# First gate weights on two hardware queues, with one x chunk on GpSimd's queue

## The chip, the cores and the metric

The kernel runs on one core of a Trainium2 chip. The metric is the device time of one execution in microseconds (us), lower is better. The kernel before takes 204.66 us (median of 5 runs, 204.03 to 205.20).

## The reference

The input x is 2048 rows of 512 (bf16). It is layer-normalized, and then two layers work on the same normalized rows; their outputs are added to x.

```python
def _B_ref(x, w1, w3, w2):              # gated layer, F = 1792
    gate = jnp.einsum("bsd,df->bsf", x, w1)
    up = jnp.einsum("bsd,df->bsf", x, w3)
    return jnp.einsum("bsf,fd->bsd", _silu(gate) * up, w2)

x = A_x
xn = _layernorm(x, axis=-1)
# _A_ref: complex state-space layer: Bu = x @ B_bar, scan h = Lam_bar * h + Bu, y = 2 Re(h @ C) + x * Dskip
return x + _A_ref(xn, ...) + _B_ref(xn, B_w1, B_w3, B_w2)
```

## The kernel before, in words

The 2048 rows are worked on in 4 blocks of 512 rows; a block is 4 chunks of 128 rows. F = 1792 is cut into 14 gate tiles of 128 columns. For a block the gated layer (`glu`) runs, for each gate tile f, four matmuls with w1 (the 512 inputs are 4 tiles of 128) and four with w3 into two PSUM tiles; ScalarE copies them out (`evac`: SiLU for the gate, a plain copy for the other), VectorE multiplies. The state-space layer (`bu`, `ssm_tasks`) and the output products (`y_fast`) follow between and behind.

Each engine runs its instructions in the order in which the program writes them. VectorE's work between the matmuls is placed by a small planner (`Filler`), whose costs and due times the change doesn't touch.

Block 0 has a start of its own, since nothing is loaded yet. Its rows come chunk by chunk, and its first three gate tiles (`FIRST` = 3) are computed chunk by chunk too, by `quarter`, line 557: `quarter(0, (0, 1), 2)` is chunk 0 with gate tiles 0 and 1, first all of w1, then all of w3, 16 matmuls of 128 columns. For each chunk, VectorE makes mean and variance (`ln_stats`, lines 214 and 215), ScalarE the inverse deviation (`ln_first_rstd`, 228 and 229), VectorE normalizes (`ln_apply`, 219), TensorE transposes (`ln_first_transpose`, 238) and ScalarE copies the transposed tile out (239). TensorE warms up before that with matmuls on constants (`keep_busy`, 191).

The order of TensorE's work in the start is written out by hand:

```python
quarter(0, (0, 1), 2)
quarter(1, (0, 1))
pps = params_transpose()
...
ln_first_transpose(2)
quarter(0, (2,))
ln_first_transpose(3)
quarter(1, (2,))
```

`params_transpose` (line 310) transposes the state-space layer's parameter rows, which GpSimd loads in three small DMAs (line 200); ScalarE and GpSimd derive small tables from them, and VectorE the angle tables (369 to 372). From gate tile 3 on, whole blocks are multiplied (line 525).

Loads: SyncE and ScalarE each issue half of x chunks 0 and 1 (line 161). Then ScalarE issues chunk 3 (162) and SyncE chunk 2 (163). `load_w(f0, f1)` loads columns f0 to f1 of w1 (line 151) and of w3 (152): first 0 to 256, gate tiles 0 and 1, then 256 to 512, gate tiles 2 and 3; all on SyncE. A load of 256 columns is 256 KB, a chunk of x 128 KB. GpSimd has a queue of its own, of the software kind, on which it also runs its accumulating DMAs. `bulk_loads` (the rest of w1 and w3, block 1 of x, the transposed loads of B and C) starts on SyncE once the first chunk's deviation is there, and `late_loads` (w2, Dskip, blocks 2 and 3 of x) come at about 33 us.

Of the kernel before, what the change touches and what calls it, by code (L numbers as in the profile page):

```python
# [17 lines left out]
P = 128  # L18
# [45 lines left out]
def kernel(  # L64
# [17 lines left out]
    nc = tc.nc  # L82
# [23 lines left out]
    xv = A_x[0].rearrange("(c p) d -> p c d", p=P)  # L106
# [39 lines left out]
    x_blk = [xpool.tile([P, CPB, D], BF16, name="x_blk") for _ in range(NBLK)]  # L146
# [3 lines left out]
    def load_w(f0, f1, eng1=nc.sync, eng3=nc.sync):  # L150
        eng1.dma_start(out=w1_sb[:, :, f0:f1], in_=w1v[:, :, f0:f1])  # L151
        eng3.dma_start(out=w3_sb[:, :, f0:f1], in_=w3v[:, :, f0:f1])

    def load_x(b, parts=1):
        n = CPB // parts
        for i in range(0, CPB, n):
            nc.sync.dma_start(out=x_blk[b][:, i:i + n, :], in_=xv[:, b * CPB + i:b * CPB + i + n, :])

    for c in range(2):
        for eng, dsl in ((nc.sync, slice(0, D // 2)), (nc.scalar, slice(D // 2, D))):  # L160
            eng.dma_start(out=x_blk[0][:, c, dsl], in_=xv[:, c, dsl])  # L161
    nc.scalar.dma_start(out=x_blk[0][:, 3, :], in_=xv[:, 3, :])
    nc.sync.dma_start(out=x_blk[0][:, 2, :], in_=xv[:, 2, :])  # L163
    load_w(0, 2 * P)
    load_w(2 * P, 4 * P)

    def bulk_loads():
# [9 lines left out]
    def late_loads():  # L177
        nc.sync.dma_start(out=w2_sb, in_=B_w2.rearrange("(t p) d -> p t d", p=P))
        nc.sync.dma_start(out=dskip_row, in_=A_Dskip.partition_broadcast(P))
        load_x(2, 4)  # L180
        load_x(3)


    ones = nc.const_aps.tensor(1.0, (P, TBLK), BF16)
# [615 lines left out]
    for t in ln1b:  # L800
        bg.add(*t, ("ln", 1))
    bg.add(0.0, late_loads, ("ln", 1))
    bg.add(0.2, params_w)
    gate = glu(0)
# [94 lines left out]
```

## Time and profile before

| | before |
|---|---|
| median of 5 runs | 204.66 us (204.03 to 205.20) |
| profiled execution, its own time | 204.66 us |
| profiled execution, span of its instructions | 202.8 us |
| TensorE (PE) busy | 198.1 us, 98% of the span |
| VectorE (DVE) busy | 172.5 us, 85% |
| ScalarE (ACT) busy | 125.4 us, 62% |
| GpSimd (POOL) busy | 41.5 us, 20% |
| granted TensorE clock | full speed in every slice |
| first w1 load: issued, landed | 2.11, 5.79 us |
| first w3 load: issued, landed | 2.58, 7.60 us |
| second w1 load and w3 load: issued | 3.13 and 3.69 us |

All times in the profile count from the start of the span. A DMA's time to landing runs from its issue to the completion that its reader waits for. `PEld` is the loading of weights into TensorE, which overlaps the matmuls; `SPq` and `ACTq` are DMA issues by SyncE and ScalarE. The DMA engines are 16, shared by all queues. Matmuls are pipelined, so a matmul's start tells more than its duration: consecutive starts of the 128-column matmuls lie about 0.056 us apart.

### The profile page before, as it was taken

How to read it: one execution, taken by the hardware profiler on the slowest of the kernel's cores; microseconds unless marked ns; L12 is line 12 of the kernel's file. 1: busy time of each engine (PE TensorE's matmuls, PEld its weight loads, DVE VectorE, ACT ScalarE, POOL GpSimd, SP SyncE). 2: the span in 40 equal slices, each digit the busy share in tenths (PEclk: the TensorE clock that was granted, in tenths of full speed). 3: DMA queues.
4: the chain of work that ended last, by engine and by line, in shares of the span. 5: the costliest groups of instructions: out<-in, count | busy, mean ns of one | idle time of the engine just before them, and what ended most of it. 6: DMA issues, size and time to landing. Idle time of an engine off the chain costs nothing.

```text
span 202.8 us, 3451 instructions
## 1 busy us (share of the span) xinstructions
PE 198.1 (98%) x1317; PEld 122.8 (61%) x1317; DVE 172.5 (85%) x242; ACT 125.4 (62%) x251; POOL 41.5 (20%) x68
## 2 busy tenths in 40 slices
PE   8899999999999999999999999999999999999994
PEld 2774444444444588854444445888444458888993
DVE  4589699999999999989949999999999935584832
ACT  4699897699999976969766676110576662101010
POOL 7070269700310043041111010310101110000000
PEclk9999999999999999999999999999999999999999
DMA  5999986992483043936796004466330780101011
GB/s 157 327 249 209 298 166 116 324 266 46 91 156 66 0 83 68 169 99 118 75 187 128 13 13 94 93 141 133 90 65 0 150 162 1 52 3 52 29 40 39
DMA packets 28816, 23.16 MB, mean 114 GB/s; under 512 B 16128, under 2 KB 26496, under 8 KB 28800
## 3 DMA queue, kind: packets, MB, share of 16 engines
q1 hardware_dynamic: 25536, 13.21, 27.2%
q0 software_dynamic: 2688, 9.44, 25.0%
q10 hardware_dynamic: 576, 0.30, 0.5%
q8 instruction: 10, 0.16, 0.3%
q14 instruction: 6, 0.05, 0.1%
HBM read 7.74 MB, written 2.10 MB: 48 GB/s over the span
## 4 chain that ended last, share of the span: by engine, by line
PE 94%; DMA 2%; SPq 1%; DVE 1%; issue 0%
PE gu_ps L525 45%; PE gu_ps L724 16%; PE y_ps L724 9%; PE bu_ps L724 7%; PE bu_ps L435 7%; PE y_ps L435 7%; DMA w_sb<-in_B_w_dram 2%; PE gu_ps L557 2%; PE bu_ps L557 1%; DVE xn L735 1%; SPq L161 0%; PE y_ps L238 0%; SPq L151 0%; DVE x_blk L735 0%; SPq L163 0%
## 5 line engine op out<-in xcount | busy, mean ns | idle before, releaser
L525 PE MATMUL gu_ps<-xnT,w_sb 128*128 128x512 bf16 x424 | 92.5, 379 | 0.0
L525 PEld LDWEIGHTS <-w_sb 128*128 128x128 bf16 x424 | 41.5, 98 | 49.3
L724 PEld LDWEIGHTS <-act 128*128 128x128 f16 x451 | 43.2, 98 | 5.5
L534 ACT ACTIVATE g<-gu_ps 128x512 bf16<-128x512 f32 x55 | 33.1, 601 | 14.3 <-PE gu_ps L525 13.7
L535 ACT ACTIVATE u<-gu_ps 128x512 bf16<-128x512 f32 x55 | 33.2, 603 | 9.9 <-PE gu_ps L525 9.5
L435 PEld LDWEIGHTS <-bt 128*128 128x128 bf16 x128 | 12.5, 98 | 15.1
L543 DVE TENSOR_TENSOR act<-g,u 128x1024 f16<-128x1024 bf16 x28 | 19.0, 678 | 3.1 <-ACT u L535 3.1
L478 DVE TENSOR_TENSOR_SCAN u<-rho,act,u 128x512 bf16<-128x512 f32 x16 | 19.6, 1268 | 0.0
L492 POOL DMA_DIRECT2D act<-p x8 | 7.1, 885 | 44.8 <-DVE act L488 30.8
L435 PE MATMUL bu_ps<-xnT,bt 128*128 128x512 bf16 x64 | 15.1, 379 | 0.0
L435 PE MATMUL y_ps<-xnT,bt 128*128 128x512 bf16 x64 | 15.1, 379 | 0.0
L457 DVE TENSOR_TENSOR p<-u,tabe 128x2048 bf16<-128x2048 bf16 x8 | 9.8, 1220 | 2.7 <-DMA act<-p 2.6
L724 PE MATMUL y_ps<-tw,act 128*128 128x256 f16 x88 | 10.9, 273 | 0.0
L437 ACT ACTIVATE u<-y_ps 128x512 bf16<-128x512 f32 x16 | 9.5, 594 | 2.3 <-PE y_ps L435 2.1
L468 POOL DMA_DIRECT2D u<-p x6 | 5.2, 874 | 27.5 <-ACT u L535 7.9
L724 PE MATMUL gu_ps<-w_sb,act 128*128 128x256 bf16 (+1 forms) x84 | 10.8, 268 | 0.0
L724 PE MATMUL gu_ps<-tw,act 128*128 128x256 f16 x88 | 10.7, 273 | 0.0
L437 ACT ACTIVATE u<-bu_ps 128x512 bf16<-128x512 f32 x16 | 9.5, 594 | 2.0 <-PE bu_ps L435 1.9
L744 ACT ACTIVATE bu_ps<-y_ps 128x256 f32<-128x256 f32 x4 | 1.5, 369 | 13.7 <-PE y_ps L724 13.7
L461 DVE TENSOR_TENSOR u<-u,tabe 128x2048 bf16<-128x2048 bf16 x8 | 9.8, 1222 | 0.2
L478 DVE TENSOR_TENSOR_SCAN u<-rho,ends,u 128x512 bf16<-128x512 f32 x8 | 9.9, 1270 | 0.0
L484 DVE TENSOR_TENSOR p<-u,tabe 128x2048 f16<-128x2048 bf16 x8 | 9.8, 1222 | 0.1
(146 smaller groups left out, 277.3 us busy)
## 6 DMA issues: line engine op xcount, KB each, us to landing
act<-p POOLq DMA_DIRECT2D x8, 512.0 KB, 4.8
u<-p POOLq DMA_DIRECT2D x6, 512.0 KB, 4.9
xn<-x_blk POOLq DMA_DIRECT2D x4, 512.0 KB, 5.8
out_dram<-xn SPq DMA_DIRECT2D x15, 128.0 KB, 1.7
w_sb<-in_B_w_dram SPq DMA_DIRECT2D x1, 1792.0 KB, 7.7
w_sb<-in_B_w_dram SPq DMA_DIRECT2D x2, 768.0 KB, 6.4
w_sb<-in_B_w_dram SPq DMA_DIRECT2D x4, 256.0 KB, 5.2
w_sb<-in_B_w_dram SPq DMA_DIRECT2D x2, 512.0 KB, 6.6
```

The source lines that it names most:

```text
L435: nc.tensor.matmul(out=ps, lhsT=bt[:, ri, dt, pt * P:(pt + 1) * P], rhs=xnT_blk[b][:, dt, :], start=(dt == 0), stop=(dt == NDT - 1))
L437: nc.scalar.activation(out=u[:, j, ri, :], in_=ps, func=ACT.Copy)
L457: nc.vector.tensor_tensor(out=st["p"][:, :, ::-1, :], in0=st["g"], in1=tabe[:, psl, 2:0:-1, :], op=ALU.mult)
L461: nc.vector.tensor_tensor(out=st["g"], in0=st["g"], in1=tabe[:, psl, 0:1, :].to_broadcast(FULL), op=ALU.mult)
L478: nc.vector.tensor_tensor_scan(out=v, data0=rho[:, pt:pt + 1].to_broadcast([P, TBLK]), data1=v, initial=init, op0=ALU.mult, op1=ALU.add)
L484: nc.vector.tensor_tensor(out=st["p16"][:, :, ::-1, :], in0=st["g"], in1=tabe[:, psl, 1:3, :], op=ALU.mult)
L492: gp.dma_start(out=act_state(b, hf), in_=st["p16"], accum_op=ALU.add)
L525: nc.tensor.matmul(out=ps[:, tsl], lhsT=w[:, dt, f * P:(f + 1) * P], rhs=xnT[:, dt, tsl], start=(dt == 0), stop=(dt == NDT - 1))
L534: nc.scalar.activation(out=g16[:, f % 2, :], in_=g_ps, func=ACT.Silu)
L535: nc.scalar.activation(out=u16[:, f % 2, :], in_=u_ps, func=ACT.Copy)
L543: nc.vector.tensor_tensor(out=act(b)[:, k0:k1 + 1:k1 - k0, :], in0=g16, in1=u16, op=ALU.mult)
L724: nc.tensor.matmul(out=out, lhsT=left[:, k, :], rhs=right[k][:, cols], start=(start and k == 0), stop=(k == NK - 1), skip_group_check=True)
```

## The change

Behind the halves of chunks 0 and 1, SyncE issues the first w1 load and ScalarE the first w3 load, side by side. Chunk 2 of x is issued by GpSimd, ahead of everything else that GpSimd does in this kernel; chunk 3 is issued by SyncE behind the first w1 load. The second pair of weight loads stays on SyncE. Block 3 of x, late in the kernel, is loaded in two pieces of two chunks in place of one.

```diff
     for c in range(2):
         for eng, dsl in ((nc.sync, slice(0, D // 2)), (nc.scalar, slice(D // 2, D))):
             eng.dma_start(out=x_blk[0][:, c, dsl], in_=xv[:, c, dsl])
-    nc.scalar.dma_start(out=x_blk[0][:, 3, :], in_=xv[:, 3, :])
-    nc.sync.dma_start(out=x_blk[0][:, 2, :], in_=xv[:, 2, :])
-    load_w(0, 2 * P)
+    nc.gpsimd.dma_start(out=x_blk[0][:, 2, :], in_=xv[:, 2, :])
+    load_w(0, 2 * P, nc.sync, nc.scalar)
+    nc.sync.dma_start(out=x_blk[0][:, 3, :], in_=xv[:, 3, :])
     load_w(2 * P, 4 * P)
 
     def bulk_loads():
@@ -178,7 +178,7 @@
         nc.sync.dma_start(out=w2_sb, in_=B_w2.rearrange("(t p) d -> p t d", p=P))
         nc.sync.dma_start(out=dskip_row, in_=A_Dskip.partition_broadcast(P))
         load_x(2, 4)
-        load_x(3)
+        load_x(3, 2)
```

## The prediction

> **What bounds the kernel now.** I read the page first, then the waits, then the chain of work in order of time, then the timelines of TensorE and VectorE over the first 13 us, and last the DMA rates by stage. From the page:
>
> ```profile
> PE 198.1 (98%) x1317; PEld 122.8 (61%) x1317; DVE 172.5 (85%) x242; ACT 125.4 (62%) x251; POOL 41.5 (20%) x68
> ...
> PE 94%; DMA 2%; SPq 1%; DVE 1%; issue 0%
> ```
>
> TensorE is busy nearly everywhere, and it carries 94% of the chain that ended last. The only other large piece is a DMA. The waits, for TensorE alone and then for all engines in the first 24 us, say where it sits:
>
> ```profile
> PE gu_ps L557 <- DMA w_sb<-in_B_w_dram: 0.9, 1, 0.9
> ...
> PEld L557 <- DMA w_sb<-in_B_w_dram: 1.1, 1, 1.1
> ```
>
> Apart from its start, this is the one recorded wait of TensorE in the whole execution. The chain in order of time (start, length, what) shows which transfer it was:
>
> ```profile
> 2.11 0.43 SPq L151
> 2.54 0.04 issue
> 2.58 5.01 DMA w_sb<-in_B_w_dram
> 7.60 0.05 issue
> 7.64 1.51 PE gu_ps L557 x24
> ```
>
> So the w3 load of the first two gate tiles, issued by SyncE at 2.58 behind w1's at 2.11, lands at 7.60; from there TensorE runs on without a gap until 198.6. Whatever moves TensorE's work after 7.64 moves the end, one for one, unless another wait appears. The timeline of TensorE shows the work that follows (start, duration, line, tiles, count):
>
> ```profile
> 6.09 0.61 PE L557 MATMUL gu_ps<-xnT,w_sb 128*128 128x128 bf16 x8
> 7.64 1.51 PE L557 MATMUL gu_ps<-xnT,w_sb 128*128 128x128 bf16 x24 [0.94 <-DMA w_sb<-in_B_w_dram]
> 9.09 0.18 PE L310 MATMUL y_ps<-ident,par_rows 12*128 12x12 bf16 x1
> 9.20 0.40 PE L238 MATMUL y_ps<-ident,xn 128*128 128x128 bf16 x4
> 9.43 0.61 PE L557 MATMUL bu_ps<-xnT,w_sb 128*128 128x128 bf16 x8
> ```
>
> The row at 6.09 is chunk 0 against w1, 8 matmuls; the row at 7.64 is chunk 0 against w3 (8) and chunk 1 against both (16). The row at 9.43 is gate tile 2: 4 matmuls with w1, 4 with w3, and they need the *second* pair of weight loads. Eight matmuls start within 0.45 us (from 10.10 to 10.55 in the same view), four within 0.22. Without its wait the w3 group would start at 6.09 + 0.45 = 6.54. The hole is 7.64 - 6.54 = 1.10 us, the 1.1 of the weight loads' wait.
>
> **The change, part by part.** The sum is made against the profiled execution: span 202.8, its own time 204.66, so 1.86 lies outside the span; 204.66 is also the median of the runs.
>
> *Issues.* SyncE issues first w1 at 1.64 in place of 2.11. ScalarE issues first w3 at 1.65, in the slot of chunk 3, in place of 2.58 on SyncE. The issue takes about 0.51 on SyncE where chunk 3 took 0.45 on ScalarE, so ScalarE's table load slips from 2.13 to 2.19 and ends at 3.47; ScalarE's next work is at 3.98. That costs nothing. SyncE has one issue less before the second pair: its w3 goes out at 3.69 - 0.56 = 3.13.
>
> *Bytes.* What decides a landing is the bytes ahead of it, and the windows show this (columns: stretch, its length, busy time and count of PE, PEld, DVE, ACT, POOL, then clock, DMA share, GB/s):
>
> ```profile
> 1.75:3.00 1.25, 1.25 (x5) 0.46 (x3) 0.03 (x1) 0.87 (x1) 1.25 (x3) 1.00 0.80 216
> 3.00:4.25 1.25, 1.25 (x5) 0.43 (x3) 1.22 (x3) 0.68 (x2) 1.18 (x3) 1.00 0.86 238
> 4.25:5.75 1.50, 1.50 (x11) 0.69 (x9) 1.35 (x6) 1.22 (x7) 0.36 (x3) 1.00 0.96 269
> 5.75:7.75 2.00, 1.06 (x17) 0.86 (x15) 1.91 (x5) 1.70 (x7) 0.00 (x0) 1.00 1.14 331
> ```
>
> The DMA engines are busy 80 to 114% of these stretches, so reordering issues redistributes the time but adds little of it. By these rates 270 kB have moved by 3.00, 567 by 4.25 and 971 by 5.75. Before, first w1 had 786 kB up to its end (four x chunks of 131 kB, itself 262), which the sum reaches at 5.06; the trace has it landed at 5.79, 0.73 later (skew between engines and completion). First w3 (1049 kB) is reached at 5.99 and landed at 7.60, 1.6 later: in the trace's semaphore counts 14 of its 16 parts were in by 6.67, the last two came at 7.18 and 7.60. In the change w1 and w3 move side by side, and with chunk 2 beside them 917 kB have to pass: 5.55, with a lag of 0.73 it is 6.28. Then TensorE starts w1 at 6.33 in place of 6.09 and w3 right behind at 6.78: 0.86 of the 1.10 is recovered. With the lag of 1.6 both land at 7.15, w3 starts at 7.65, and nothing is recovered here. The parts' own times put most engines at the small lag, and I take 6.3 to 6.8 for w3.
>
> The Trainium skill, "DMA: Bandwidth & Descriptors", section "Issuing engines are not separate DMA queues", speaks against the change: DMAs of all issuers share the same 16 engines, and several issuers save only sequencer time. The rates above agree: 238 GB/s while both hardware queues carried x, 269 and 331 later with nearly all on SyncE's. By the rule alone the change is worth at most the earlier issue, 0.93 us of w3.
>
> *What is late next.* With the hole gone, the parameter transpose could start at 7.99, the transposes of chunk 2 at 8.10, gate tile 2 with w1 at 8.33, with w3 at 8.55. The latter needs the second w3 load. It was issued at 3.69 with this time to landing:
>
> ```profile
> DMA to landing us min/median/max: 5.6/5.6/5.6
> ```
>
> That is 9.34, and tile 2's w3 matmuls started at 9.43 + 0.22 = 9.65, so before it landed just in time, hidden by the first wait. All bytes ahead of it are the same after the change. If it lands at 9.34 again, they start at 9.39: the gain is 0.26, not 1.10. If its 0.56 earlier issue came through in full, 8.78, the gain would be 0.82. I take 9.2 to 9.3, close to the first end, since the engines were busy when the issue was made: gain about 0.35.
>
> *Chunk 2 on GpSimd's queue.* No large plain load from GpSimd is in the trace. Near rows: three 1 KB loads at 3.5 to 4.0 us to landing, 512 KB accumulating ones at 4.8 to 5.8. From issue at 0.72 this is 4.2 to 6.5. VectorE asks for it at 5.61:
>
> ```profile
> 5.61 0.69 DVE L214 BATCH_NORM_STATS2 stats<-x_blk 128x6 f32<-128x512 bf16 x1
> ...
> 6.43 0.66 DVE L214 BATCH_NORM_STATS2 stats<-x_blk 128x6 f32<-128x512 bf16 x1
> ```
>
> I take 4.7, nearer to the small rows since it is 128 KB: no cost. At 6.5 VectorE would be 0.9 late, normalization of chunk 2 would end at 8.65 instead of 7.75, still before the 9.20 at which its transposes run now. Chunk 3, behind w1 on SyncE, comes 131 kB later, some 6.7; its statistics slip from 6.43 by 0.3, also inside that cover. GpSimd itself is held 0.5 to 0.9 by the issue (its issues took 0.50 to 0.88): ident is ready near 2.2 (first needed 4.97), the parameter rows land by 7.3 to 7.65 instead of 6.75 (needed 7.99 at the earliest).
>
> *Block 3 in two pieces.* One more SyncE issue of about 0.5 at 37 us; SyncE's next is at 77.92. Nothing.
>
> Sum: hole -1.10, of it 0.75 given back at the second w3 load: 204.66 - 0.35 = 204.3. About 0.3%, or 0.6 us, is what a measurement of this kernel can tell from no change, so I forecast no change that can be told.
>
> **The rivals.**
>
> *The whole hole closes.* The two slow parts of w3 came during one stretch (5.79 to 7.60); the second w3 load had 14 of 16 parts at 8.35. If no engine straggles this time, it lands by 8.5, and gain is 0.82 to 1.10: 203.56 to 203.84. For it: earlier issues, and that before's runs reach down to 204.03. Against: the lag of about 1 us is still there at the next load.
>
> *The second w3 load comes later (slower).* Chunk 2 now puts 131 kB on the software queue, and the parameter rows' packets move 0.5 to 0.9 later, into the time of the second pair. If this doubles the lag of the last parts from 1.0 to 2.0, it lands at 10.3, tile 2 starts at 10.37 in place of 9.65: +0.7, 205.4. It decides from a landing after 9.60. For it: the rate is lowest (216 to 238) while several queues carry data. Against: the parameter rows are tiny, and chunk 2 should be through before 5. The same page, section "Latency and other measured facts", says that two of the sixteen engines are usually slower and suspects the software queue's descriptor rings; this trace has two late parts of sixteen, but no run here shows which engines.
>
> *Nothing arrives at the end.* VectorE (85%) or ScalarE absorbs the shift later: 204.66. Against: their start, too, hangs on the parameter transpose, which moves with TensorE.
>
> **How the numbers follow.** The likeliest, wait moved to the second w3 load: 0.42, range 203.9 to 204.5. Hole closed: 0.33. Slower: 0.20. Absorbed: 0.05. Faster than 204.05 is the second case and a part of the first, 0.38; slower than 205.27 is the slow case with its upper part and a little of others, 0.18; the rest 0.44. Range 203.5 to 205.3.
>
> **What would show it.** Right: TensorE's wait before L557 gone or under 0.3 in chunk 0, a new one of 0.5 to 0.9 before the bu_ps group of L557, released by w_sb; the first matmul of L525 at 12.9 in place of 13.23. Closed hole: L525 at 12.1 to 12.4. Slower: L525 after 13.8. Wrong altogether: a wait of the transposes of chunk 2 on x_blk, or a new TensorE wait after 14 us.

## The result and the profile after

The changed kernel takes 204.77 us (median of 40 runs, 204.33 to 205.29) against 204.25 (75 runs, 203.49 to 205.73) for the kernel before, run on the same chips. The ratio is 1.0023 [1.0015, 1.0031]: slower by 0.23%, about 0.5 us, small but outside its interval. The forecast was 0.35 us the other way, from 204.66 (the median of 5 runs) to 204.3: no change that can be told. 204.77 lies inside the range given, but the sign and the mechanism behind the likeliest case are not what happened. Of the 0.52 us between the medians, 0.13 lies outside the span of instructions (1.97 against 1.84, medians over the runs) and the rest inside it.

The profiled execution of the changed kernel has a span of 202.8 us and a time of its own of 204.75. The page again shows TensorE nearly always busy; a different transfer is in the chain that ended last:

```profile
PE 197.9 (98%) x1317; PEld 122.6 (60%) x1317; DVE 173.0 (85%) x242; ACT 125.4 (62%) x251; POOL 42.1 (21%) x69
...
PE 93%; DMA 3%; POOL 1%; issue 1%; DVE 1%; POOLq 0%
```

The waits of TensorE name it (line and what was waited for; us in total, times, longest):

```profile
PE bu_ps L191 <- PEq L883: 0.8, 1, 0.8
PE y_ps L238 <- POOL mhalf L204: 0.7, 1, 0.7
PE y_ps L310 <- DMA par_rows<-in_A_Lambda_im_dram: 0.4, 1, 0.4
```

The 0.9 us before L557 on the weights is gone, as the change intends. (The 0.8 on PEq is the start of the program and stands in the profile of before too.) Two new waits stand in its place: the first transposes (L238) and the parameter transpose (L310). For L238 the profile names GpSimd's last memset, but the weight loads of the same transposes wait 1.3 for VectorE's normalization (L219), which an experiment below takes up. The forecast wait, of the bu_ps group of L557 on `w_sb`, does not exist. The chain in order of time, at the head of the kernel (start, length, what):

```profile
1.28 0.06 POOL x_blk L162
...
2.63 1.01 POOL par_rows L200 x2
3.64 5.27 DMA par_rows<-in_A_Lambda_im_dram
8.91 0.14 issue
9.05 0.16 PE y_ps L310
9.21 0.33 PE y_ps L238 x4
```

The end now hangs on the last of three 1 KB loads of parameter rows: issued by GpSimd at 3.64, behind chunk 2 of x at 1.28, and 5.27 us on its way. In the profile of before the same load was issued at 2.77 and landed at 6.75, 4.0 us on its way, long before TensorE asked for it. The timeline of TensorE over the same stretch:

```profile
5.55 0.54 PE L238 MATMUL y_ps<-ident,xn 128*128 128x128 bf16 x4 [0.74 <-POOL mhalf L204]
...
6.68 1.96 PE L557 MATMUL gu_ps<-xnT,w_sb 128*128 128x128 bf16 x32
9.05 0.16 PE L310 MATMUL y_ps<-ident,par_rows 12*128 12x12 bf16 x1 [0.40 <-DMA par_rows<-in_A_Lambda_im_dram]
9.14 0.40 PE L238 MATMUL y_ps<-ident,xn 128*128 128x128 bf16 x4
9.38 0.61 PE L557 MATMUL bu_ps<-xnT,w_sb 128*128 128x128 bf16 x8
...
13.17 1.67 PE L525 MATMUL gu_ps<-xnT,w_sb 128*128 128x512 bf16 x7
```

Both w1 and w3 are there when their matmuls begin, so all 32 of L557 (chunks 0 and 1) run in one piece. But they begin at 6.68 and not at 6.09, and the parameter transpose behind them waits until 9.05. Against the profile of before, where it ran at 9.09: hole -1.10, later beginning +0.59, wait for the rows +0.47 (32 starts 0.056 apart from 6.68 end at 8.47, and 0.11 passes to the next, as before), together -0.04. The first matmul of L525 is at 13.17 in place of 13.23: in these two profiled executions the head is equal.

The medians differ nevertheless, because the profiled execution of before was not a typical one: 204.66 where the median is 204.25. Its first w3 load landed at 7.60. In the profiles of the four variants below that keep the order of the hardware queues' loads as it was and chunk 2 on SyncE's queue, the load landed at 6.66 to 7.00, no matmul is recorded waiting for weights in any of them (TensorE's weight loads wait 0.3 in two), and in three of the four L525 starts at 12.41 to 12.64 (in the fourth the rows delayed it). A typical head of before is thus 0.4 us shorter, by the medians of the times, to 0.8, by these profiles, than the one in which the prediction filled a hole.

The DMA rates by stage (columns: stretch, length, PE, PEld, DVE, ACT, POOL, clock, DMA share, GB/s) answer to those of before:

```profile
1.75:3.00 1.25, 1.25 (x5) 0.44 (x3) 0.00 (x0) 0.89 (x1) 1.17 (x5) 1.00 0.99 234
3.00:4.25 1.25, 1.25 (x5) 0.42 (x3) 1.10 (x3) 0.52 (x2) 1.24 (x4) 1.00 0.61 162
4.25:5.75 1.50, 0.76 (x5) 0.14 (x3) 1.47 (x5) 1.05 (x5) 1.22 (x4) 1.00 1.05 312
5.75:7.75 2.00, 2.00 (x31) 1.70 (x30) 1.89 (x5) 1.64 (x5) 0.00 (x0) 1.00 1.18 317
```

From 3.00 to 7.75, 1305 kB moved (before 1363): nothing was sped up, only dealt out differently. First w3 landed at 6.41 and first w1 at 6.64, where before had w1 at 5.79.

### The profile page after: what moved, and what is told of

Same layout as the page of the kernel before. It is cut to its first block, busy times and chain, and to the rows that moved or that the text cites. A ratio compares the mean times of both kernels' runs of the same rounds, so it can differ in the third digit from the quotient of the medians.

```text
span 202.8 us, 3452 instructions
## 1 busy us (share of the span) xinstructions
PE 197.9 (98%) x1317; PEld 122.6 (60%) x1317; DVE 173.0 (85%) x242; ACT 125.4 (62%) x251; POOL 42.1 (21%) x69
## 4 chain that ended last, share of the span: by engine, by line
PE 93%; DMA 3%; POOL 1%; issue 1%; DVE 1%; POOLq 0%
PE gu_ps L525 45%; PE gu_ps L724 16%; PE y_ps L724 9%; PE bu_ps L724 7%; PE bu_ps L435 7%; PE y_ps L435 7%; DMA par_rows<-in_A_Lambda_im_dram 3%; PE bu_ps L557 1%; PE gu_ps L557 1%; DVE xn L735 1%; POOL par_rows L200 1%; PE y_ps L238 0%; DVE x_blk L735 0%; POOL ident L197 0%; PE y_ps L310 0%
## 5 line engine op out<-in xcount | busy, mean ns | idle before, releaser
L525 PE MATMUL gu_ps<-xnT,w_sb 128*128 128x512 bf16 x424 | 92.5, 379 | 0.0
L525 PEld LDWEIGHTS <-w_sb 128*128 128x128 bf16 x424 | 41.5, 98 | 49.3
```

The lines of the kernel that those rows point to most:

```text
L525: nc.tensor.matmul(out=ps[:, tsl], lhsT=w[:, dt, f * P:(f + 1) * P], rhs=xnT[:, dt, tsl], start=(dt == 0), stop=(dt == NDT - 1))
```

## The experiments

The expectations name theories by letters of their own. The question moved in three steps: is the loss due to chunk 2 on GpSimd's queue or to something else in the change; why does a 1 KB load land 2 us later for one more load ahead of it on its queue; and what is left if that is mended.

**Chunk 2 back on SyncE, behind first w1.** (Wherever chunk 2 goes back to SyncE below, block 3 is loaded in one piece as before.)

```diff
-    nc.gpsimd.dma_start(out=x_blk[0][:, 2, :], in_=xv[:, 2, :])
     load_w(0, 2 * P, nc.sync, nc.scalar)
+    nc.sync.dma_start(out=x_blk[0][:, 2, :], in_=xv[:, 2, :])
     nc.sync.dma_start(out=x_blk[0][:, 3, :], in_=xv[:, 3, :])
```

> The changed kernel with chunk 2 issued by SyncE between the first w1 load and chunk 3, so that GpSimd starts as before (block 3 of x in one piece again, which keeps the number of hardware DMAs). Theory A (the change loses through GpSimd: its issue of chunk 2 moves the parameter rows' landing from 6.75 to 8.91 and TensorE waits for them): the wait before L310 is gone, the rows land at 6.5 to 7.0, the first L525 matmul starts at 12.2 to 12.5 in place of 13.17, time 203.7 to 204.0, faster than the changed kernel by 0.8 to 1.0. Theory B (the order and the sharing of the weight loads is what costs): the time stays at 204.4 to 204.8, with a wait for w_sb.

204.57 (12 runs), ratio 1.0021 [1.0004, 1.0038]. A miss on the time: a loss where a gain was expected. The rows now land at 7.29 and the wait of L310 is gone, but behind two weight loads chunk 2 itself is late. VectorE's timeline and then TensorE's:

```profile
6.55 0.69 DVE L214 BATCH_NORM_STATS2 stats<-x_blk 128x6 f32<-128x512 bf16 x1 [0.84 <-DMA x_blk<-in_A_x_dram]
```

```profile
7.97 0.18 PE L310 MATMUL y_ps<-ident,par_rows 12*128 12x12 bf16 x1
8.61 0.40 PE L238 MATMUL y_ps<-ident,xn 128*128 128x128 bf16 x4 [0.46 <-DVE xn L219]
```

So this run removes one wait and makes another. The position of chunk 2 matters too, and not only its queue. How much, this execution doesn't show: it took 204.11, 0.46 less than the median, with L525 at 12.69.

**Chunk 2 ahead of the weights, on SyncE.** The change's weights keep their two queues; only chunk 2 leaves GpSimd.

```diff
-    nc.gpsimd.dma_start(out=x_blk[0][:, 2, :], in_=xv[:, 2, :])
+    nc.sync.dma_start(out=x_blk[0][:, 2, :], in_=xv[:, 2, :])
     load_w(0, 2 * P, nc.sync, nc.scalar)
```

> The changed kernel with chunk 2 issued by SyncE, ahead of the first w1 load, so that it lands near 4.5 and GpSimd starts as before (block 3 in one piece). Theory A: neither parameter rows nor chunk 2 are late; rows at 7.3 to 8.1, first w1 and w3 both by 6.6, first L525 at 12.2 to 12.6, time 203.7 to 204.1, faster than before by 0.1 to 0.5. Theory B: w1 or w3 lands after 7.2 and the time is 204.4 to 204.8.

204.18 (11), ratio 1.0002 [0.9989, 1.0015]. The rows land at 7.46, no wait at L310, and what is left is the weights:

```profile
PE gu_ps L557 <- DMA w_sb<-in_B_w_dram: 0.4, 1, 0.4
```

First w3 and w1 land at 6.40 and 6.80. The loss is gone; so is every gain: the two weights side by side, the very core of the change, bring nothing that can be told. Against the four variants named above, w3 comes 0.3 to 0.6 earlier, but w1 0.7 to 1.1 later (theirs landed at 5.68 to 6.14).

**Only chunk 2 to GpSimd, nothing else.**

```diff
-    nc.sync.dma_start(out=x_blk[0][:, 2, :], in_=xv[:, 2, :])
+    nc.gpsimd.dma_start(out=x_blk[0][:, 2, :], in_=xv[:, 2, :])
```

> The kernel before with nothing changed but that chunk 2 is issued by GpSimd, ahead of its other work; chunk 3 stays on ScalarE and all weights on SyncE. Theory A: this part alone costs what the whole change costs: parameter rows at 8.7 to 9.0, a wait before L310, first L525 near 13.2, time 204.7 to 204.9. Theory B (the weight loads' order costs): 204.0 to 204.3, as before or faster, since first w1 and w3 come earlier by the bytes of chunk 2.

204.73 (12), ratio 1.0033 [1.0018, 1.0048]. One line of the change, applied to the kernel before, costs as much as the whole. The wait is the same:

```profile
PE y_ps L310 <- DMA par_rows<-in_A_Lambda_im_dram: 0.6, 1, 0.6
```

**The rows on SyncE, chunk 2 left on GpSimd.** This is the opposite test: the suspected victim leaves the queue. Block 2 of x is loaded in two pieces and block 3 in one, since the three small loads add to SyncE's.

```diff
     nc.sync.dma_start(out=x_blk[0][:, 3, :], in_=xv[:, 3, :])
+    for i, src in enumerate((A_log_dt, A_Lambda_re, A_Lambda_im)):
+        nc.sync.dma_start(out=par_rows[i * NPT:(i + 1) * NPT, :], in_=src.rearrange("(t p) -> t p", p=P))
     load_w(2 * P, 4 * P)
...
-        load_x(2, 4)
-        load_x(3, 2)
+        load_x(2, 2)
+        load_x(3)
...
-    for i, src in enumerate((A_log_dt, A_Lambda_re, A_Lambda_im)):
-        nc.gpsimd.dma_start(out=par_rows[i * NPT:(i + 1) * NPT, :], in_=src.rearrange("(t p) -> t p", p=P))
```

> The changed kernel, chunk 2 still on GpSimd's queue, but the three parameter rows issued by SyncE behind chunk 3 (blocks 2 and 3 of x late in the kernel in two pieces and in one, which keeps the number of hardware DMAs). Theory C (the rows, which wait their turn on GpSimd's queue, pin the start): they land at 7.0 to 7.5, no wait before L310, first L525 at 12.4 to 12.8, time 204.1 to 204.4. Theory E (chunk 2's own turn on the DMA engines, ahead of parts of chunk 1 and of the weights, is what costs): rows early, but chunk 1 or the weights late, time 204.6 to 204.9.

204.05 (12), ratio 1.0001 [0.9992, 1.0009]. TensorE's timeline has no wait at L310 and the earliest L525 but one of all these kernels:

```profile
6.42 1.96 PE L557 MATMUL gu_ps<-xnT,w_sb 128*128 128x128 bf16 x32 [0.17 <-DMA w_sb<-in_B_w_dram]
8.32 0.18 PE L310 MATMUL y_ps<-ident,par_rows 12*128 12x12 bf16 x1
...
12.46 0.81 PE L525 MATMUL gu_ps<-xnT,w_sb 128*128 128x512 bf16 x2
```

The loss is gone with chunk 2 still on GpSimd's queue. Together with the two runs before, this shows the cause: it is the parameter rows that stand behind chunk 2 on that queue. It is also the best that any form of the change did: the kernel before, no more (its 32 runs beside this one have a median of 204.09).

**How long a small load takes in that queue.** Three kernels put one, two or three unused 1 KB loads ahead of the rows in the kernel *before*; nothing else is changed, chunk 2 stays on SyncE.

```diff
+    extra = const.tile([NPT, P], BF16, name="extra")
+    nc.gpsimd.dma_start(out=extra, in_=A_Lambda_im.rearrange("(t p) -> t p", p=P))
     for i, src in enumerate((A_log_dt, A_Lambda_re, A_Lambda_im)):
```

> The kernel before with a fourth 1 KB load on GpSimd's queue, ahead of the three parameter rows; its data are not used. Theory C: the last row moves one hardware DMA back, from behind the first w3 load to behind the second w1 load, 7.7 to 8.7 in place of 6.75, about 0.1 to 0.4 behind that load's landing; TensorE's wait for w3 covers most of it, time 204.0 to 204.8. Theory D: the row moves by the issue of the extra load alone, 0.5 to 0.7, to 7.2 to 7.5.

> The kernel before with two more 1 KB loads on GpSimd's queue ahead of the three parameter rows; their data are not used. No byte of x or of the weights moves otherwise. Theory C: the last row lands two hardware DMAs later than before, behind the second w3 load, at 8.8 to 9.6; TensorE waits for it, first L525 at 12.9 to 13.5, time 204.6 to 205.0: the whole loss of the change from 2 KB. Theory E: the loss needs chunk 2's bytes; 204.0 to 204.3.

> The kernel before with three more 1 KB loads on GpSimd's queue ahead of the parameter rows (two landed the last row at 8.38, just as TensorE got there). Theory C: the last row takes one more turn and lands behind the third w1 load, at 9.9 to 10.6; TensorE waits 1.4 to 2.1 for it, first L525 at 14.0 to 14.8, time 205.4 to 206.2, all of it from 3 KB. Rival (the rows' landing is set by GpSimd's issue, 0.5 to 0.55 per load, and a latency of some 4.6): the last row at 8.9 to 9.1, time 204.5 to 204.8.

The landings of the last row load, read from the trace:

| ahead of the three rows | issued | landed | weight load that landed nearest | wait at the parameter transpose | median us |
|---|---|---|---|---|---|
| nothing (before) | 2.77 | 6.75 | first w3, 14 of its 16 parts by 6.67 | none | 204.25 (75 runs) |
| one 1 KB load | 3.29 | 8.14 | second w1, 8.02 | none | 204.04 (1) |
| two | 3.75 | 8.38 | second w3, 8.46 | 0.2 | 204.11 (11) |
| three | 4.26 | 8.75 | second w3, 8.52 | 0.5 | 204.70 (12) |
| chunk 2 of x (alone) | 3.64 | 8.98 | second w3, 8.75 | 0.6 | 204.73 (12) |
| chunk 2 of x (the change) | 3.64 | 8.91 | second w3, 8.69 | 0.4 | 204.77 (40) |

With three ahead, the wait is on the page of waits in the same form as with the change (lines of that kernel are shifted by 3):

```profile
PE y_ps L313 <- DMA par_rows<-in_A_Lambda_im_dram: 0.5, 1, 0.5
```

One 1 KB load ahead delays the issue by 0.52 but the landing by 1.39: the theory that the row moves by the issue alone (7.2 to 7.5) fails. (Each line's landings are those of one execution. In two more, the kernels below with first w3 on ScalarE and with block 3 in two pieces, GpSimd's queue is as before and the last row landed at 7.04 and 7.07, not 6.75; from there it is 1.1.) In the traces each load on GpSimd's queue lands in step with a load of the hardware queues, in most cases 0.1 to 0.3 behind it: in the change the rows come at 7.15, 8.06 and 8.91, behind chunk 3 at 6.91, second w1 at 7.81 and second w3 at 8.69. By this theory of turns, another load ahead pushes the last row behind the next weight load. GpSimd's issues themselves took no longer (0.50 to 0.57 for the three rows in the change, 0.50 to 0.74 before).

The turns are not strict, and here the stronger form of that theory missed twice: with two ahead no time is lost, since the row lands as TensorE comes for it (about 8.35), and with three ahead the ratio is 1.0037 [1.0014, 1.0060], 0.5 us and not 1.2 to 2, because the row did not wait for the next large load, which landed at 10.12; the second w3 was the last of its group. The rival of that run, a fixed latency of some 4.6 behind the issue, came close (8.9 to 9.1 for the landing, 204.5 to 204.8 for the time): the last row took 4.85, 4.63 and 4.49 with one, two and three small loads ahead. It doesn't fit the rest: 4.0 to 5.1 over the six kernels with nothing ahead on the queue, by how the hardware loads lie, 5.2 to 5.6 behind chunk 2, and 4.83 behind chunk 2 when only a hardware load is cut in two (next run). So turns are the better account, not a proven one.

The table also says that the loss doesn't need chunk 2's bytes: three loads of 1 KB cost as much time as one of 128 KB. But they do it by a later issue (4.26 against 3.64), and chunk 2 by a longer way. It gives the size: the loss begins between a landing at 8.4 and one at 8.7.

The Trainium skill, "DMA: Bandwidth & Descriptors", section "Queues, rings and completion order", has every DMA engine go round its queues packet by packet, about 9 to 17 descriptors and at most 64. The turns agree; how much is one turn is more than the typical figure: the landings in the change go by about one whole weight load, 0.85 to 0.91 us, per 1 KB load, and such a load is 512 packets of 512 bytes in the trace, 32 for each engine.

**The second w1 load in two halves.** If turns go by loads, smaller loads ahead mean shorter turns.

```diff
-    load_w(2 * P, 4 * P)
+    for t in (slice(0, 2), slice(2, 4)):
+        nc.sync.dma_start(out=w1_sb[:, t, 2 * P:4 * P], in_=w1v[:, t, 2 * P:4 * P])
+    nc.sync.dma_start(out=w3_sb[:, :, 2 * P:4 * P], in_=w3v[:, :, 2 * P:4 * P])
```

> The changed kernel with the second w1 load as two DMAs of 128 KB in place of one of 256 KB (block 3 in one piece, which keeps the number of hardware DMAs). Theory C (a sharper form of A: each DMA engine takes the queues in turn, one whole DMA of each, so that every DMA on GpSimd's queue lands just behind one hardware DMA, as they all do in the traces so far, 0.1 to 0.4 behind): the third parameter row now lands behind the second half of w1, near 8.0 to 8.2 in place of 8.9; the wait before L310 is gone, first L525 at 12.5 to 12.8, time 204.1 to 204.4. Theory D (the rows are late by GpSimd's later issue and by the bytes ahead of them, which are the same here): they land at 8.8 to 9.0 and the time is 204.7 to 204.8.

204.35 (12), ratio 1.0023 [1.0001, 1.0044]. The three rows land at 7.67, 8.02 and 8.47: the last one 0.27 behind the second half (8.20) and ahead of second w3 (8.81), where in the change it came behind it. That is the order that theory C expects and later than its 8.0 to 8.2; theory D's 8.8 to 9.0 fails. The wait was to go; it shrinks to 0.3:

```profile
PE y_ps L312 <- DMA par_rows<-in_A_Lambda_im_dram: 0.3, 1, 0.3
```

By the profile over half the loss goes (L525 at 12.73, between 12.46 and 13.17). The time doesn't show it: the ratio is the change's own, and its interval leaves open whether all or none of the loss is gone.

**The parameter transposes later in TensorE's order.** If only the position of the wait matters, other work can fill it.

```diff
             quarter(1, (0, 1))
+            ln_first_transpose(2)
+            quarter(0, (2,))
             pps = params_transpose()
             params_dt(pps)
             params_turn()
             table_angles(0)
             table_angles(1)
-            ln_first_transpose(2)
-            quarter(0, (2,))
```

> The changed kernel with the same DMAs, but with the transpose of the parameter rows (and what ScalarE, GpSimd and VectorE derive from it) placed behind the transposes of chunk 2 and gate tile 2 of chunk 0. Theory A (in the changed kernel TensorE stands still for the parameter rows, which land at 8.9): that wait goes, transposes of chunk 2 at 8.4 to 8.6, tile 2 with w3 at 8.7 to 9.0, first L525 at 12.5 to 12.8 in place of 13.17, time 204.1 to 204.4. Theory B (the weight loads' order and sharing cost): a wait for w_sb of the same size takes the place, time 204.7 to 204.8.

204.87 (11), ratio 1.0032 [1.0019, 1.0045]. A miss. The wait of L310 is gone, as meant, but L525 starts at 13.24 all the same. In this execution the weights are later: first w3 landed at 7.30 (6.41 in the change's profile) and second w3 at 9.39 (8.69), and TensorE's 32 matmuls of L557 take 2.23 in place of 1.96, the 8 of gate tile 2 0.78 in place of 0.61. Gate tile 2, moved ahead of the rows' transpose, asks for second w3 earlier and in this execution doesn't find it there. From L525 to the last matmul it is 186.62 against 186.39 in nearly all other profiles. The 0.23 more is one stop at 76.45, where line 724 waits for VectorE (`act`, L766); that the tables which hang on the rows, now later, cause it was not tried. So why the time is no better stays open: one execution with late weights doesn't show it for the median, and this run doesn't confirm that the wait at L310 alone is the loss.

**GpSimd's copy on VectorE.** In the change, GpSimd's iota and its cast (L201, L202) come later and fall beside VectorE's first `ln_apply`. The rows of line 219 from 4 to 6 us (duration in ns: min, median, max), before and then after:

```profile
L219 DVE TENSOR_SCALAR xn<-x_blk,mv_all,rstd_all x3: 316/341/413, 4.6 to 5.3; 128x256 bf16<-128x256 bf16 x2, 128x512 bf16<-128x512 bf16 x1
```

```profile
L219 DVE TENSOR_SCALAR xn<-x_blk,mv_all,rstd_all x3: 334/402/739, 4.8 to 5.7; 128x256 bf16<-128x256 bf16 x2, 128x512 bf16<-128x512 bf16 x1
```

One of the applies took 739 ns in place of 316. The engines' timeline of after shows beside what:

```profile
4.75 1.32 DVE L219 TENSOR_SCALAR xn<-x_blk,mv_all,rstd_all 128x256 bf16<-128x256 bf16 x3
4.80 0.61 POOL L202 CAST tw<-tw 128x512 f32<-128x512 int32 x1
```

```diff
-    nc.gpsimd.tensor_copy(out=iota_f, in_=iota_i)
...
+            nc.vector.tensor_copy(out=iota_f, in_=iota_i)
```

> The changed kernel with the integer-to-float copy of the iota row (L202) done by VectorE behind the normalizations of block 0 in place of by GpSimd at 4.80. Tests the first apply of VectorE, which took 739 ns beside GpSimd's copy and 316 ns before. Theory A, with the two engines getting in each other's way: the apply is back at 300 to 350 ns and the first transposes start at 5.1 to 5.2 in place of 5.55; the time stays at 204.7 to 204.8 all the same, because the parameter rows still land at 8.9. Theory B, in which the long apply comes from something else (data still arriving): it stays above 600 ns.

204.88 (8), ratio 1.0044 [1.0027, 1.0060]. The applies are back at 314 to 412 ns, the transposes start at 5.06, and the time is what it was: TensorE then waits 0.7 us, not 0.4, for the same row, which lands at 8.89. This slowdown is real (two variants with GpSimd's work in the same order, chunk 2 alone to GpSimd and second w1 in halves, have one apply at 631 and 634 beside the cast), but what comes behind it is set by the rows. The Trainium skill, "SBUF — State Buffer", section "Terms", says that VectorE and GpSimd share a port pair which one of them locks for a whole instruction; the 0.42 us that the apply lost beside the 0.61 us cast, and got back without it, agree. Not every VectorE instruction is hit: in the kernel before, the same cast (3.92 to 4.53) ran beside the statistics of chunk 1 (L214, 3.80 to 4.47), which took 0.67 there as elsewhere.

**Chunk 2 behind the rows, on GpSimd.**

```diff
-    nc.gpsimd.dma_start(out=x_blk[0][:, 2, :], in_=xv[:, 2, :])
...
     for i, src in enumerate((A_log_dt, A_Lambda_re, A_Lambda_im)):
         nc.gpsimd.dma_start(...)
+    nc.gpsimd.dma_start(out=x_blk[0][:, 2, :], in_=xv[:, 2, :])
```

> The changed kernel with GpSimd issuing chunk 2 behind the three parameter rows in place of ahead of everything. Theory A: the rows land near 6.75 and the wait before L310 goes; chunk 2 lands near 6.8 and its statistics wait some 0.8, so the transposes of chunk 2 become the late ones at 8.6 to 9.0; first L525 at 12.7 to 13.0, time 204.3 to 204.6. Theory B: no change against the changed kernel, 204.7 to 204.8, since the same bytes move.

208.08 (6), ratio 1.0184 [1.0154, 1.0214]: the wait moved where it was expected, the time was missed by far, and it is slower than the changed kernel where a gain on it was expected. Issued at 3.29, chunk 2 landed at 8.84, 0.37 behind second w3 (8.47). The wait went to its transposes:

```profile
PE y_ps L238 <- DVE xn L219: 2.6, 1, 2.6
```

In the profiles, L525 starts 3.45 later than in the changed kernel (16.62 against 13.17), and 1.79 of it is there when these transposes start (10.93 against 9.14). The windows (columns as above) show the rest, in the clock:

```profile
8.00:10.93 2.93, 0.32 (x6) 0.13 (x3) 1.93 (x5) 0.79 (x3) 0.00 (x0) 1.00 1.10 347
10.93:14.00 3.07, 3.07 (x38) 3.03 (x39) 2.06 (x5) 2.91 (x7) 2.13 (x7) 0.67 1.19 285
14.00:18.00 4.00, 4.00 (x44) 3.29 (x43) 2.60 (x6) 2.36 (x6) 2.24 (x7) 0.83 1.16 181
```

After the pause, TensorE was granted 0.67 and 0.83 of its clock. From the transposes of chunk 2 to L525 it took 16.62 - 10.93 = 5.69, where the changed kernel takes 13.17 - 9.14 = 4.03: 1.66 us more. Finer windows give 0.84 from 10.93 to 12.50, 0.50 to 14.00, 0.53 to 15.50 and 1.00 behind; what is missing to full speed in them adds up to 1.7 us (an estimate), so the clock accounts for all of it. The Trainium skill, "TensorE: Matmul & The Clock Gate", section "Part 1: The HAM clock gate", halves the clock after at least one idle window of about 3.4 us; here 2.61 us of recorded idling was enough. In the changed kernel, with waits of 0.74 and 0.40, the clock is 1.00 in every window shown.

**First w3 alone on ScalarE.** The change's first idea by itself, in the kernel before (chunk 3 stays ahead of it).

```diff
-    load_w(0, 2 * P)
+    load_w(0, 2 * P, nc.sync, nc.scalar)
```

> The kernel before with nothing changed but that the first w3 load is issued by ScalarE behind chunk 3. All theories of the loss: GpSimd and chunk 2 untouched, so no loss; if the DMA engines take whole DMAs in turn, w1 and w3 move in nearly the same order as before and the time is that of before, 204.0 to 204.3. If an earlier issue of w3 alone were worth something, 203.5 to 203.9. ScalarE's table load ends 0.5 later, at 3.9, just ahead of its first use at 4.0.

204.53 (12), ratio 1.0018 [0.9996, 1.0040]: inconclusive. The head of its profile is as good as any (L525 at 12.52), but that execution (206.29) holds a wait of 2.0 us at L525 for a DMA that belongs to the layer norm of a later block, and it is no sample of the median. It gives no sign of a gain.

**Block 3 in two pieces, alone, and taken back.**

```diff
-        load_x(3)
+        load_x(3, 2)
```

> The kernel before with nothing changed but that block 3 of x is loaded in two pieces. All theories: one more issue at 37 us, where SyncE has nothing else to do until 78; no difference, 204.0 to 204.3.

> The changed kernel with block 3 of x in one piece as before, all else as changed. It separates the two parts of the loss: the start (wait for the rows: stays, first L525 near 13.2) and what lies outside the span (1.97 in the changed kernel, 1.84 before). If the split of block 3 causes the latter, it returns to 1.80 to 1.86 and the time is 204.6 to 204.75; if not, it stays at 1.95 to 2.0 and the time is 204.75 to 204.9. The final waits on SyncE may grow by 0.07, since the last store then has the semaphore that is waited for last but one.

In the kernel before: 204.60 (8), ratio 1.0025 [1.0015, 1.0035]. No theory expected a difference. The head is a good one (L525 at 12.41); the loss is at the end. From the start of the last matmul to the end of the span it is 3.61, where all the other kernels have 3.18 to 3.27. The trace shows SyncE at line 894 waiting for all DMA semaphores in turn, about 0.065 us for each check. Its waits there, in the kernel before and then here (us in total, times, longest):

```profile
SPq L894 <- DMA out_dram<-xn: 0.7, 2, 0.5
```

```profile
SPq L894 <- DMA out_dram<-xn: 1.2, 1, 1.2
```

With one load more, the semaphore of the last store is the second in that row: SyncE gets through at 201.08 and has seven checks still to make, until 201.52. In the kernel before it is late in the row, and most checks are done while the store runs. The time outside the span, 1.84 before, is 2.00 here; 0.4 and 0.16 make the loss of 0.5 within what the medians can tell.

In the changed kernel this end takes 3.22, for there SyncE and ScalarE together issue one load less at the start. Taking the split back there gave 204.83 (6), against 204.77 with it: the time outside the span went from 1.97 to 1.82, the median span from 202.8 to 203.0, and the time did not fall. So the split is no shown part of the change's loss. Over all runs (medians), the time outside the span is 1.97 to 2.03 in the five kernels that load block 3 in two pieces and 1.82 to 1.85 in the others, but 2.01 in the run with first w3 on ScalarE, where nothing is split; what sets it stays open, and with it the 0.13 us that the change has there.

## Why the prediction was wrong

**What held.** First w3 at 6.3 to 6.8: 6.41, though 6.74 to 7.30 in four other profiles that issue the first weights in the same way. Chunk 2 at 4.7: 4.77, no wait; this is partly luck, since it was issued at 1.28 and not 0.72, and took 3.49 and not 4.0. Chunk 3 at 6.7: 6.91, no wait. The wait before L557 gone. A shift of TensorE's early work carried to the end: from L525 to the last matmul it is 186.38 to 186.39 in most of the profiles, before and after among them. And the rule weighed against the change, that all issuers share the engines, agrees with what the weights did: side by side on two queues they bring nothing that can be told (204.18 against 204.14 for the kernel before beside it).

**The step that failed: GpSimd's queue.** The prediction looked for the cost of chunk 2 on that queue in chunk 2, and for the rows it added the later issue, 0.5 to 0.9, to the old landing: "the parameter rows land by 7.3 to 7.65". The issue moved by 0.87, as forecast; the landing by 2.16, to 8.91 (by 1.8 from the 7.04 and 7.07 of the two other executions). The larger part is not the issue but the place in the queue: behind one more load, the last row comes behind second w3, and TensorE waits 0.4 to 0.7 for it. The rival that looked at "the parameter rows' packets" had them slow down the weights; by the order of the landings, the weights slowed the rows. The prediction had the time at which TensorE would ask for them (7.99 at the earliest) and the nearest rows (3.5 to 4.0 us to landing), but those were measured with nothing large ahead on the same queue. Moving the rows off the queue removed the loss; putting chunk 2 alone on it made it.

**The hole was taken from one execution.** 1.10 us was right for that profile, and wrong for the median: a first w3 load at 7.60 was late by 0.6 to 0.9 against 6.66 to 7.00 in four profiles with the same order. The prediction saw the two late parts of sixteen, but took the hole that they made as what every execution has to give back, from a median of 5 runs that was 0.4 above that of 75. With recorded waits for the weights of 0.3 or none in place of 1.1, and first w1 later, there was next to nothing to win: the two variants of the change in which neither the rows nor chunk 2 came late take as long as before (204.18 and 204.05).

**First w1 was mis-sized.** The matmuls of L557 were to start at 6.33; they started at 6.68, with w1 at 6.64 (5.79 before, 6.28 by the sum of bytes). Beside w3 and chunk 2 it gives up what w3 gains. Which of the two comes first is not fixed: in the four other profiles w1 landed at 5.85 to 6.73 and w3 at 6.74 to 7.30. The later of the two, at 6.64 to 7.30, is no earlier than first w3 in the old order, 6.66 to 7.00. Part of the later start is VectorE's: the transposes ahead of L557 began at 5.55 in place of 4.98. VectorE's apply at 739 ns was not in the sum at all: GpSimd's later work was costed only by its issues, not by what its copy then stands beside. Without it the time was the same.

**What was expected to be late next was not.** Second w3 was given 9.2 to 9.3, "close to the first end"; it landed at 8.69, near the other end (8.78), and no TensorE wait for it is recorded. In the profiles the hole was given back elsewhere: 0.59 by the later beginning and 0.47 by the wait for the rows.

**Block 3 in two pieces: "nothing".** At its place, yes. Alone it costs 0.5 us, at the kernel's last line; in the change no cost of it could be told.

## What to carry to other kernels

A load put on a queue is paid by what stands behind it there: list every later load of that queue with the time at which its reader asks, and do not carry over its old time to landing, least of all for small loads on a queue that shares the engines with large ones. Two loads side by side on two issuers trade one's landing for the other's. Before filling a hole, ask how it lies in several executions: here the profiled run, 0.4 us above the median, held a hole that the usual run hardly has.

## What the runs showed of the hardware

- On GpSimd's queue a 1 KB load took 3.5 to 4.0 us to land before and 4.6 to 5.3 in the change, behind chunk 2, and one more 1 KB load ahead cost the last of them 1.1 to 1.4 us; in most cases they land 0.1 to 0.3 behind a load of the hardware queues. 128 KB took 3.49 us as the first load of that queue (1.28 to 4.77) and 5.55 us behind three small ones (3.29 to 8.84).
- Behind a pause of 2.61 us TensorE's granted clock was 0.67 and 0.83 of full speed over the next stretches, worth 1.66 us.
- VectorE's apply took 739 ns beside a GpSimd cast, 314 to 316 ns without it; its statistics took 0.67 us beside the cast as elsewhere.
- One load more on the hardware queues changed the order in which the last line waits for the semaphores: 0.4 us at the end of the kernel.
